# Sparse attention and two expert layers in one kernel: one run of value matmuls per group and head pair, shared turns of the last keys, and later weights moved by DMA before they are turned

## The chip, the core and the metric

One core of one Trainium2 chip runs the whole kernel. The metric is the device time of one execution in microseconds (us). The engines are named as in the profile: PE (matrix products; PEld is its weight load), DVE, ACT, POOL and SP. DVE, ACT and POOL work elementwise, and SP issues every DMA of this kernel, one after the other.

## What is computed

Batch 2, 8 heads, 576 tokens, head size 64, all fp32. Each row of scores keeps its 32 largest.

```python
scores = scale * np.matmul(q, k.transpose(0, 1, 3, 2))
kth = np.partition(scores, -32, axis=-1)[..., -32:-31]
scores = np.where(scores >= kth, scores, -1e9)
attn = softmax(scores)                      # by rows, 1e-9 added to the sum
x = (attn @ v)                              # heads side by side: 1152 x 512
x = sum(p[:, e:e+1] * (relu(x @ w1[e]) @ w2[e]) for e in range(4))    # 512 -> 1024 -> 512
out = ((x @ w_a) * (x @ w_b)) @ w_out       # 512 -> 1536 -> 512
```

## The kernel before

The 1152 tokens are nine tiles of 128: four of each batch (512 tokens), and one, `MIX`, with the last 64 tokens of both. The tiles form four groups of 1, 2, 3 and 3 tiles, called groups 0 to 3 here. The attention is done group by group, in a group by head pair (4 of them), in a head pair by tile: 36 steps, each of one tile and two heads. Steps 0 to 3 are group 0, 4 to 11 group 1, 12 to 23 group 2, 24 to 35 group 3.

A step does this. PE makes the scores of the two heads (`scores`), ACT copies them out of PSUM (L703). DVE finds the 32 largest of each row in four rounds of eight, MAX8 (L723) with MATCH_REPLACE8 between them (L731), which writes the tile `e`. Then POOL (L748), ACT (L754), POOL (L758), ACT (L762), POOL (L767), DVE (L770) and ACT (L773) make the softmax weights in `e`. `weigh` turns each head's weights on PE (L461) in five pieces: four of 128 keys and one of the last 64, whose turned form has 64 partitions. ACT copies the turned weights out of PSUM into a slot of `pts` in two instructions (L828, L832). Last, PE multiplies them with v, ten products of fp32 (each two PE instructions) for a tile; the two heads write the two halves of the 128 partitions, so these matmuls have 64 weight columns, and the trace shows their shape as 128*64. The products of the last 64 keys read `vrem`. After a group's last tile of a head pair, ACT and DVE copy the result to `xs` (L866, L868).

As soon as all head pairs of a group are done, its expert layer can begin (`plain` for group 0, `experts` for the others). An expert weight unit is loaded to `raw`, split into two fp32r parts by ACT (L889) and POOL or DVE (L890) into `mid`, and used by PE; ACT (L959) and DVE (L963, L988) take the results out. The last layer (`gated`) follows when all groups are through.

The order on every engine is worked out before the launch by a planner (`Plan`). Each operation has an engine, an assumed duration, a key (the smallest goes first among those that could run), what it waits for, and the slots of memory that it holds. Attention has keys near its step's number and the expert layers keys above 500 (for PE above 1000), so expert work fills what attention leaves free. The order found is emitted as it stands, one queue per engine, so a waiting instruction holds up everything behind it on that engine; that goes for SP's DMAs too. Copies out of PSUM for the expert layers have key -1000 and go before the search for the largest.

Slots that matter here: `e` has six of one head each, so three steps; `pt` has three of one head each; `raw` and `w` have four weight units each. Nothing of the weights is moved by DMA before the change. Turns of q and k are fp32r, turns of the weights are fp32.

Of the kernel before, what the change touches and what calls it, by code (L numbers as in the profile page):

```python
# [319 lines left out]
TURN_R, TURN_F, TOP, REPLACE = 88, 109, 662, 732  # L320
LATE = 2

FILL = 9
SLACK = 1200

# [3 lines left out]
def body(tc, q, k, v, probs, w1, w2, wa, wb, wo, out):  # L329
# [55 lines left out]
    krem = [big.t[0:REM, b * 1024:(b + 1) * 1024].rearrange("p (h a d) -> p h a d", a=2, d=D) for b in range(B)]  # L385
    big.at = 2048
# [4 lines left out]
    big.at = 2048  # L391
# [5 lines left out]
    low = Region("low", 12300, F32)  # L397
# [4 lines left out]
    es = low.slots("e", 6, S)  # L402
    pts = low.slots("pt", 3, (M4 + 1) * 128)
# [117 lines left out]
    krem_done, vrem_done, qrem_done, kept = {}, {}, [], {}  # L521

    def keys(b, h2, key, eng):
# [11 lines left out]
        if b not in krem_done:  # L535
            rr = krraws.tile(key)
            rrv = lambda: rr.ap[0:REM].rearrange("p (h d) -> p h d", d=D)

            krem_done[b] = {}
            for h0, h1 in ((0, 2), (2, H)) if first_ else ((0, H),):  # L540
                l2 = load(
                    lambda h0=h0, h1=h1: rrv()[:, h0:h1], lambda h0=h0, h1=h1: last_rows(k, b)[:, h0:h1],
                    key - 1.98 if h1 == 2 else key - 1.9, (), [rr], 16384 * (h1 - h0),
                )
                d = split(
                    lambda h0=h0, h1=h1: krem[b][:, h0:h1, 0], lambda h0=h0, h1=h1: krem[b][:, h0:h1, 1],
                    lambda h0=h0, h1=h1: rrv()[:, h0:h1], 64 * (h1 - h0), key + (0.01 if h0 == 0 else 0.05), [l2], [rr], eng,
                )
                krem_done[b].update({i: d for i in range(h0, h1)})
        got = []  # L550
        for j in range(2):
            at = atts.tile(key + 0.02 + 0.01 * j)

            def turn(j=j, at=at):
                p = at.ap.bitcast(F32R)
                for m in range(M4):
                    tr(p[:, 0, m * 128:(m + 1) * 128], sv()[:, j, m].rearrange("p a d -> p (a d)"), identr)
                tr(p[:, 1, 0:REM], krem[b][:, h + j].rearrange("p a d -> p (a d)"), identr[0:REM, 0:REM])

            o = tensor(640, turn, key + 0.02 + 0.01 * j, sp[j] + krem_done[b][h + j] + [ready], [at, st_])  # L560
            if first_ and j == 1:
                got.append(vector(
                    dve(S),
                    lambda j=j, at=at: nc.vector.tensor_copy(kt.ap[:, j * S:(j + 1) * S], at.ap.rearrange("p a n -> p (a n)")[:, 0:S]),
                    -902 + j, [o], [at, kt],
                ))
                continue
            got.append(scalar(
                S,
                lambda j=j, at=at: nc.scalar.activation(  # L570
                    kt.ap[:, j * S:(j + 1) * S], at.ap.rearrange("p a n -> p (a n)")[:, 0:S], AF.Copy
                ),
                -902 + j, [o], [at, kt],
            ))
# [14 lines left out]
    def start_pair(c, h2, n):  # L589
# [74 lines left out]
        for b in batches(tiles):  # L664
            vt = vts.tile(n)
            pair.v[b] = vt
            pair.vd[b] = [load(
                lambda vt=vt: vt.ap.rearrange("p (h m d) -> p h m d", h=2, m=M4), lambda b=b: main_rows(v, b, h), n - 2.5, (), [vt], since=9e3 + 3e3 * n,
            )]
            if b not in vrem_done:  # L670
                vrem_done[b] = load(lambda b=b: vrem[b][0:REM], lambda b=b: last_rows(v, b), n - 2.4, (), (), 131072, since=14e3)
# [36 lines left out]
    def masked(sd, n):  # L708
# [5 lines left out]
        e = [es.tile(n) for _ in range(2)]  # L714
        last, firsts = [], []

        def top(x, src, c0, rounds, width, key, done):

            for r in range(rounds):
# [4 lines left out]
                    [m8, sd[x][0], e[x]],  # L724
# [3 lines left out]
                if r < rounds - 1:  # L728
                    done = vector(
                        132 + 1.04 * width,  # L730
                        lambda at=at, cs=cs: nc.vector.match_replace(  # L731
                            out=src[1](), in_to_replace=m8v()[:, x, cs], in_values=at(), imm_value=LOW
                        ),
                        key + 0.02 * r + 0.01, [done], [m8, sd[x][0], e[x]],
                    )
            return done

        for x in range(2):
            s = sd[x][0]
            key = n + (0.4 if urgent else 0.001) * x  # L740
            last.append(top(x, [lambda s=s: s.ap, lambda x=x: e[x].ap], 0, TOPK // 8, S, key, sd[x][1]))
# [8 lines left out]
        for x in range(2):  # L750
# [3 lines left out]
                S, lambda x=x, s=s: nc.scalar.activation(e[x].ap, s.ap, AF.Relu, bias=endv()[:, x, 1:2], scale=-STEEP),  # L754
                ks, [en], [s, e[x], ends], sbuf=True, ptr=True,
            )
            b = gpsimd(
                pool_(S), lambda x=x, s=s: nc.gpsimd.tensor_tensor(e[x].ap, s.ap, e[x].ap, op=ALU.subtract), ks, [a], [s, e[x]]  # L758
# [4 lines left out]
                    e[x].ap, e[x].ap, AF.Exp, bias=endv()[:, x, 0:1], scale=scale, accum_out=sums.ap[:, x:x + 1]  # L763
                ),
                ks, [b], [e[x], ends, sums], sbuf=True, ptr=True, extra=92,
# [5 lines left out]
        for x in range(2):  # L771
            out_.append((e[x], scalar(
                S, lambda x=x: nc.scalar.activation(e[x].ap, e[x].ap, AF.Copy, scale=sums.ap[:, x:x + 1]),  # L773
                ks, [rc], [e[x], sums], sbuf=True, ptr=True,
            )))
        return out_

    def hurried(sd, n, m8v, m8, ends, endv, sums, firsts, last):

        out_ = []  # L780
        for x in range(2):
            s, e = sd[x][0], es.tile(n)
# [5 lines left out]
                S, lambda x=x, s=s, e=e: nc.scalar.activation(e.ap, s.ap, AF.Exp, bias=endv()[:, x, 0:1], scale=scale),  # L788
# [4 lines left out]
            def mask(x=x, s=s, e=e, sv=sv):  # L793
                nc.vector.scalar_tensor_tensor(  # L794
                    e.ap, s.ap, m8v()[:, x, TOPK - 1:TOPK], e.ap, op0=ALU.is_ge, op1=ALU.mult, accum_out=sv()
# [3 lines left out]
                nc.vector.tensor_scalar(e.ap, e.ap, sv(), None, op0=ALU.mult)  # L799

            out_.append((e, vector(1450, mask, -3000, [ex, last[x]], [s, e, m8, sums], port=True)))
        return out_
# [3 lines left out]
    def weigh(pair, i, ed, n):  # L806

        t, T = pair.tiles[i], pair.T
        if i == 0:
            pair.o, pair.od = os_.tile(), []  # L810
        ov = lambda: pair.o.ap[:, 0:T * 128].rearrange("p (t c) -> p t c", c=128)
        pt, ptd = [], []
        for e, done in ed:

            kt = n + (-0.45 if n == URGENT else 0.5)
            at, p = atts.tile(kt), pts.tile(n)

            def turn(e=e, at=at):
                a = at.ap.rearrange("p b (m c) -> p (b m) c", c=128)
# [4 lines left out]
            o = tensor(4 * TURN_F + 80, turn, kt, [done, ready], [at, e])  # L824

            def ev0(at=at, p=p):
                a = at.ap.rearrange("p b (m c) -> p (b m) c", c=128)
                nc.scalar.activation(p.ap[:, 0:MAIN].rearrange("p (m c) -> p m c", c=128), a[:, 0:M4], AF.Copy)  # L828

            def ev1(at=at, p=p):  # L830
                a = at.ap.rearrange("p b (m c) -> p (b m) c", c=128)
                nc.scalar.activation(p.ap[0:REM, MAIN:MAIN + 128], a[0:REM, M4], AF.Copy)  # L832

            ke = -3000 if n == URGENT else -900
            ptd.append(scalar(512, ev0, ke, [o], [at, p]))
            ptd.append(scalar(128, ev1, ke, [o], [at, p]))
            pt.append(p)
        groups = [(0, 128, t[0])] if t != MIX else [(b * REM, (b + 1) * REM, b) for b in range(B)]
        bs = [b for _, _, b in groups]

        def emit():

            for r0, r1, b in groups:
                for m in range(M4 + 1):
                    for j in range(2):
                        vt = pair.v[b].ap.rearrange("p (h m d) -> p h m d", h=2, m=M4)
                        l = vt[:, j, m] if m < M4 else vrem[b][:, pair.h + j]
                        mm(
                            ov()[j * D:(j + 1) * D, i, r0:r1], l, pt[j].ap[:, m * 128 + r0:m * 128 + r1],
                            start=(m == 0), stop=(m == M4),  # L850
                        )

        pair.od.append(tensor(
            1245, emit, n + 0.6, [zeroed] + ptd + sum((pair.vd[b] for b in bs), []) + [vrem_done[b] for b in bs], [pair.o] + pt + [pair.v[b] for b in bs]
        ))
# [380 lines left out]
```

## Time and profile before

| | |
|---|---|
| time, median of 3 runs | 841.81 us (841.73 to 843.05) |
| span of the profiled execution | 838.8 us |
| what lies around the span, against the median | 3.0 us |
| PE busy | 816.7 us, 97% |
| PEld busy | 730.4 us, 87% |
| DVE busy | 702.5 us, 84% |
| ACT busy | 540.0 us, 64% |
| POOL busy | 265.7 us, 32% |
| DMA queue | 116.17 MB, 43.9% of 16 engines |
| mean granted PE clock | 0.997 |

The span runs from the first to the last instruction of the profiled execution; that execution's own time is its span and what lies around it, taken here as the 3.0 us between span and median. Busy time is a mean over stages with different limits: the attention's steps end about half way through, and what is left is PE work.

### The profile page before, as it was taken

To read this page: it belongs to the slowest core of one execution; us is meant where nothing else is said; L and a number is where in the kernel's file an instruction comes from. 1 tells how busy PE (TensorE), PEld (TensorE's weight loads), DVE (VectorE), ACT (ScalarE), POOL (GpSimd) and SP (SyncE) were. 2 spreads that over 40 slices of the span, in tenths; PEclk is the share of its full clock that TensorE was granted. 3 is DMA by queue.
4 is the path that set the end of the run, shared out by engine and by line. 5 is a ranking of instruction groups with operands and counts; after the bars stand their busy time and mean duration, and the time that the engine had idled before them with its cause. 6 is when DMAs were issued, how large, how long until landed. Compare 5 with 4: busy or idle time off the path is not lost.

```text
span 838.8 us, 14118 instructions
## 1 busy us (share of the span) xinstructions
PE 816.7 (97%) x5177; PEld 730.4 (87%) x5177; DVE 702.5 (84%) x1363; ACT 540.0 (64%) x1037; POOL 265.7 (32%) x250
## 2 busy tenths in 40 slices
PE   7599999999999999999999999999999999999997
PEld 6477877789898999899989998999898989999996
DVE  7999999999999999999969998545235888899723
ACT  6888887989999989887666556343125535344220
POOL 3634443797998966763110000000000000000000
PEclk9999999999999999999999999999999999999999
DMA  5849977754555435233335656433002322323003
GB/s 176 286 120 313 308 240 236 218 175 165 192 172 178 148 138 182 84 95 101 101 126 169 208 158 220 126 125 101 1 1 63 89 78 73 101 78 100 26 1 113
DMA packets 83509, 117.06 MB, mean 140 GB/s; under 512 B 10608, under 2 KB 54640, under 8 KB 83440
## 3 DMA queue, kind: packets, MB, share of 16 engines
q1 hardware_dynamic: 83440, 116.17, 43.9%
q8 instruction: 40, 0.66, 0.3%
q14 instruction: 29, 0.24, 0.1%
HBM read 109.07 MB, written 7.08 MB: 138 GB/s over the span
## 4 chain that ended last, share of the span: by engine, by line
PE 80%; DVE 14%; ACT 4%; issue 1%; POOL 0%; DVEq 0%; POOLq 0%; ACTq 0%
PE ps L458 76%; DVE low L723 7%; DVE low L731 6%; PE ps L461 5%; ACT mid L889 1%; ACT low L773 1%; ACT low L762 1%; ACT low L703 0%; ACT low L828 0%; ACT low L754 0%; ACT big L514 0%; ACT big L655 0%; DVE low L794 0%; POOL low L758 0%; DVE low L1175 0%
## 5 line engine op out<-in xcount | busy, mean ns | idle before, releaser
L723 DVE MAX8 low<-low 128x8 f32<-128x576 f32 x288 | 203.3, 745 | 2.8 <-ACT low L703 2.6
L458 PE MATMUL ps<-xs,mid 128*128 128x384 f32 (+1 forms) x1152 | 204.6, 320 | 0.3 <-DVE mid L963 0.2
L458 PE MATMUL ps<-mid 128*128 128x512 f32 x768 | 196.8, 394 | 0.0
L458 PEld LDWEIGHTS ps<-xs,mid 128*128 128x128 f32 x1152 | 184.9, 188 | 9.1 <-DVE xs L1024 0.5
L458 PEld LDWEIGHTS ps<-mid 128*128 128x128 f32 x768 | 140.0, 188 | 22.6
L731 DVE MATCH_REPLACE8 low<-low 128x576 f32<-128x576 f32 x216 | 159.1, 741 | 0.0
L458 PE MATMUL ps<-xs,big 128*128 128x384 f32 x864 | 152.6, 335 | 0.0
L458 PEld LDWEIGHTS ps<-xs,big 128*128 128x128 f32 x864 | 150.2, 188 | 1.5 <-DVE xs L1024 0.3
L889 ACT ACTIVATE mid<-raw 128x1024 fp32r<-128x1024 f32 x96 | 101.7, 1062 | 44.4 <-PE ps L458 33.9
L890 POOL TENSOR_TENSOR mid<-raw,mid 128x1024 fp32r<-128x1024 f32 x48 | 115.2, 2407 | 13.8 <-ACT mid L889 9.5
L758 POOL TENSOR_TENSOR low<-low 128x576 f32<-128x576 f32 x70 | 99.6, 1438 | 31.9 <-ACT low L754 30.4
L890 DVE TENSOR_TENSOR mid<-raw,mid 128x1024 fp32r<-128x1024 f32 x48 | 59.3, 1236 | 24.6 <-ACT mid L889 24.1
L959 ACT ACTIVATE mid<-ps 128x384 fp32r<-128x384 f32 (+1 forms) x96 | 43.8, 457 | 52.5 <-PE ps L458 51.5
L458 PE MATMUL ps<-big,mid 128*128 128x512 f32 x324 | 76.1, 391 | 0.0
L458 PEld LDWEIGHTS ps<-big,mid 128*128 128x128 f32 x324 | 60.5, 188 | 12.6 <-DVE low L1175 0.6
L963 DVE SCALAR_TENSOR_TENSOR mid<-ps,mid 128x384 fp32r<-128x384 f32 (+1 forms) x96 | 48.3, 505 | 25.0 <-ACT mid L959 24.6
L1154 ACT ACTIVATE low<-ps 128x384 f32<-128x384 f32 x36 | 17.7, 492 | 69.7 <-PE ps L458 69.3
L773 ACT ACTIVATE low<-low 128x576 f32<-128x576 f32 x70 | 51.3, 774 | 12.1 <-DVE low L770 12.0
L762 ACT ACTIVATE low<-low 128x576 f32<-128x576 f32 x70 | 54.4, 778 | 2.2 <-POOL low L758 2.1
L461 PE MATMUL ps<-identr,low 128*128 128x128 f32 (+1 forms) x360 | 50.6, 283 | 4.7 <-ACT low L773 4.0
L754 ACT ACTIVATE low<-low 128x576 f32<-128x576 f32 x70 | 52.3, 776 | 4.3 <-POOL low L748 4.3
L703 ACT ACTIVATE low<-ps 128x576 f32<-128x576 f32 x72 | 46.6, 650 | 11.4 <-POOL low L758 7.5
(90 smaller groups left out, 1024.8 us busy)
## 6 DMA issues: line engine op xcount, KB each, us to landing
raw<-in_moe_w_dram SPq DMA_DIRECT2D x122, 512.0 KB, 3.8
big<-kscr SPq DMA_DIRECT2D x20, 576.0 KB, 5.5
low<-in_v_dram SPq DMA_DIRECT2D x24, 256.0 KB, 3.9
low<-in_moe_w_a_dram SPq DMA_DIRECT2D x12, 512.0 KB, 4.3
low<-in_moe_w_b_dram SPq DMA_DIRECT2D x12, 512.0 KB, 3.8
low<-in_moe_w_out_dram SPq DMA_DIRECT2D x12, 512.0 KB, 3.6
kscr<-big SPq DMA_DIRECT2D x8, 576.0 KB, 4.7
ys<-in_moe_w_dram SPq DMA_DIRECT2D x6, 512.0 KB, 5.2
```

The lines of the kernel that those rows point to most:

```text
L458: nc.tensor.matmul(out, l, r, **kw)
L461: nc.tensor.transpose(out, a, i)
L703: S, lambda: nc.scalar.activation(s.ap.rearrange("p (c n) -> p c n", c=2), at.ap[:, :, 0:HALF], AF.Copy),
L723: 62 + 1.04 * width, lambda at=at, cs=cs: nc.vector.max(m8v()[:, x, cs], at()), key + 0.02 * r, [done],
L731: lambda at=at, cs=cs: nc.vector.match_replace(out=src[1](), in_to_replace=m8v()[:, x, cs], in_values=at(), imm_value=LOW),
L754: S, lambda x=x, s=s: nc.scalar.activation(e[x].ap, s.ap, AF.Relu, bias=endv()[:, x, 1:2], scale=-STEEP),
L758: pool_(S), lambda x=x, s=s: nc.gpsimd.tensor_tensor(e[x].ap, s.ap, e[x].ap, op=ALU.subtract), ks, [a], [s, e[x]]
L762: lambda x=x: nc.scalar.activation(e[x].ap, e[x].ap, AF.Exp, bias=endv()[:, x, 0:1], scale=scale, accum_out=sums.ap[:, x:x + 1]),
L773: S, lambda x=x: nc.scalar.activation(e[x].ap, e[x].ap, AF.Copy, scale=sums.ap[:, x:x + 1]),
L889: hi = scalar(1024, lambda: nc.scalar.activation(u.ap[:, 0:1024], r.ap, AF.Copy), 500 + s, [ld], [u, r], sbuf=True)
L890: sub = lambda eng: eng.tensor_tensor(u.ap[:, 1024:2048], r.ap, u.ap[:, 0:1024], op=ALU.subtract)
L963: lambda h=h, p=p: nc.vector.scalar_tensor_tensor(h.ap[:, n:2 * n], p.ap[:, 0:n], 0.0, h.ap[:, 0:n], op0=ALU.max, op1=ALU.subtract),
```

## The change

- The two heads' weights of a step lie in one tile of 1152 columns. The second head's keys are put in another order, its last 64 first (in `keys` too), so that the last 64 keys of both heads are neighbours and are turned together: nine turns for a step, all of 128 columns, and two copies out of PSUM (128x512 and 128x640) in place of four.
- `vrem` holds v of the last keys in the upper partitions for even heads and in the lower ones for odd heads, and zeros elsewhere; a product of the last keys now runs over 128 partitions. Its load is two DMAs of 64 KB.
- The products with v are no longer emitted tile by tile but for all tiles of a group and head pair together, after the last of them.
- From step 8 on (`MOVED`), the weights of a step are moved by two DMAs of 288 KB, one for each head, from `e` into a slot of the new fp32r buffer `er`, and turned from there as fp32r.
- `e` has three slots of two heads (as much memory as before), `pt` four of two heads, `er` two. `er` lies over `krem` and `kspl`, of which the planner lets it have a slot when the keys are done, and the weights of the last layer come there after it.

```diff
+AV, SWITCH = 1092, 350
+MOVED = 8
...
+    ers = big.slots("er", 2, 2 * S)
+    ers.rank = 0.5
...
-    es = low.slots("e", 6, S)
-    pts = low.slots("pt", 3, (M4 + 1) * 128)
+    es = low.slots("e", 3, 2 * S)
+    pts = low.slots("pt", 4, 2 * S)
...
-            nc.gpsimd.memset(vrem[b][REM:128], 0.0)
-        for p in pts.aps:
-            nc.gpsimd.memset(p[REM:128, MAIN:MAIN + 128], 0.0)
+            for j in range(2):
+                nc.gpsimd.memset(vrem[b][(1 - j) * REM:(2 - j) * REM, j::2], 0.0)
...
-                tr(p[:, 1, 0:REM], krem[b][:, h + j].rearrange("p a d -> p (a d)"), identr[0:REM, 0:REM])
+                r = p[:, 0, MAIN - REM:MAIN] if j else p[:, 1, 0:REM]
+                tr(r, kremv(b)[:, h + j].rearrange("p a d -> p (a d)"), identr[0:REM, 0:REM])
...
+        (e, done), p, ptd = ed, pts.tile(n), []
+        f, idt = e, ident
+        if n >= MOVED:
+            f, idt = ers.tile(n), identr
+            done = [load(
+                lambda j=j: f.ap[:, j * S:(j + 1) * S].bitcast(F32), lambda j=j: e.ap[:, j * S:(j + 1) * S], n + 0.1, [done[j]], [e, f], S * 512,
+            ) for j in range(2)]
...
+                if j:
+                    tr(a[:, MAIN - 128:MAIN], f.ap[:, MAIN:MAIN + 128], idt)
                 for m in range(M4):
-                    tr(a[:, m], e.ap[:, m * 128:(m + 1) * 128], ident)
-                tr(a[0:REM, M4], e.ap[:, MAIN:S], ident)
+                    c0 = j * (S + REM) + m * 128
+                    tr(a[:, j * MAIN + m * 128:j * MAIN + (m + 1) * 128], f.ap[:, c0:c0 + 128], idt)
...
+        pair.turned.append((t, p, ptd))
+        if i < T - 1:
+            return
...
-        pair.od.append(tensor(
-            1245, emit, n + 0.6, [zeroed] + ptd + ...
+        pair.od = [tensor(
+            T * AV + SWITCH, emit, n + 0.6, [zeroed] + sum((d for _, _, d in pair.turned), []) + ...
```

## Rows read from the trace of the kernel before

**Rows 1.** The page's busy tenths in 40 slices of 21 us each.

```profile
PE   7599999999999999999999999999999999999997
...
DVE  7999999999999999999969998545235888899723
```

**Rows 2.** The chain that ended last, in order of time: start, us, what.

```profile
435.15 42.63 PE ps L458 x247
...
479.62 137.13 PE ps L458 x696
```

**Rows 3.** The timeline of PE, end of group 2's attention: start, us, what, count.

```profile
276.69 0.52 PE L458 MATMUL ps<-xs,mid 128*128 128x256 f32 x3
277.13 1.10 PE L458 MATMUL ps<-low 128*64 128x128 f32 x16
...
282.94 0.52 PE L458 MATMUL ps<-xs,mid 128*128 128x256 f32 x3
283.29 2.90 PE L458 MATMUL ps<-mid 128*128 128x512 f32 x12
286.03 1.25 PE L461 MATMUL ps<-identr,low 128*128 128x128 f32 x10
287.04 1.64 PE L458 MATMUL ps<-mid 128*128 128x512 f32 x6
...
289.67 1.09 PE L458 MATMUL ps<-low 128*64 128x128 f32 x16
...
290.92 1.33 PE L458 MATMUL ps<-big,qm 128*128 128x288 f32 x8
292.08 0.63 PE L461 MATMUL ps<-identr,big 128*128 128x128 f32 x6
292.55 0.93 PE L458 MATMUL ps<-mid 128*128 128x512 f32 x3
...
293.78 2.85 PE L458 MATMUL ps<-xs,mid 128*128 128x384 f32 x15
```

**Rows 4.** The timeline of PE, products with v of the last step.

```profile
436.47 0.69 PE L458 MATMUL ps<-low 128*64 128x64 f32 x16
436.99 0.29 PE L458 MATMUL ps<-low,vrem 128*64 128x64 f32 x4
437.11 0.64 PE L458 MATMUL ps<-low 128*64 128x64 f32 x16
437.57 0.29 PE L458 MATMUL ps<-low,vrem 128*64 128x64 f32 x4
437.79 1.65 PE L458 MATMUL ps<-mid 128*128 128x512 f32 x6
```

**Rows 5.** The timelines of DVE, POOL and ACT, weights of step 23.

```profile
270.19 1.41 DVE L723 MAX8 low<-low 128x8 f32<-128x576 f32 x2
...
273.33 0.21 POOL L748 TENSOR_TENSOR low<-low,facs 128x4 f32<-128x4 f32 x1
...
284.72 1.43 ACT L773 ACTIVATE low<-low 128x576 f32<-128x576 f32 x2
```

**Rows 6.** The timeline of all engines, weights of step 11.

```profile
132.14 0.20 POOL L748 TENSOR_TENSOR low<-low,facs 128x4 f32<-128x4 f32 x1 [2.01 <-DVE low L770]
...
141.14 1.44 ACT L773 ACTIVATE low<-low 128x576 f32<-128x576 f32 x2 [0.75 <-DVE low L770]
```

**Rows 7.** DMA issues by line: count, KB each, median us to landing.

```profile
big<-kscr SPq DMA_DIRECT2D x20, 576.0 KB, 5.5
...
low<-in_v_dram SPq DMA_DIRECT2D x24, 256.0 KB, 3.9
...
out_dram<-low SPq DMA_DIRECT2D x8, 256.0 KB, 2.0
```

**Rows 8.** The timelines of PE (turns of step 15) and DVE (step 18).

```profile
198.61 0.71 PE L461 MATMUL ps<-identr,low 128*128 128x128 f32 x5
...
201.37 0.76 DVE L723 MAX8 low<-low 128x8 f32<-128x576 f32 x1 [0.79 <-ACT low L703]
```

More of the change, by code (lines that the diff above doesn't have):

```diff
@@ L384, in body @@
     big = Region("big", 10752, F32R)
-    krem = [big.t[0:REM, b * 1024:(b + 1) * 1024].rearrange("p (h a d) -> p h a d", a=2, d=D) for b in range(B)]
-    big.at = 2048
+    krems = big.slots("krem", B, 1024)
     kspls = big.slots("kspl", 1, 2 * M4 * 2 * D)
@@ L390, in body @@
     qts = big.slots("qt", 2, 3 * 256)
-    big.at = 2048
+    big.at = 0
+    ers = big.slots("er", 2, 2 * S)
+    ers.rank = 0.5
     mid = Region("mid", 4 * 2048 + 5 * 768, F32R)
@@ L396, in body @@
     wraws = raw.slots("wraw", 4, 1024)
-    low = Region("low", 12300, F32)
+    low = Region("low", 12300 + 4 * 1152 - 3 * 640, F32)
     kraws = low.slots("kraw", 2, 2 * M4 * D)
@@ L521, in body @@
     krem_done, vrem_done, qrem_done, kept = {}, {}, [], {}
+    krem = [krems.tile(b) for b in range(B)]
+    kremv = lambda b: krem[b].ap[0:REM].rearrange("p (h a d) -> p h a d", a=2, d=D)
     def keys(b, h2, key, eng):
@@ L556, in turn @@
                 for m in range(M4):
-                    tr(p[:, 0, m * 128:(m + 1) * 128], sv()[:, j, m].rearrange("p a d -> p (a d)"), identr)
-                tr(p[:, 1, 0:REM], krem[b][:, h + j].rearrange("p a d -> p (a d)"), identr[0:REM, 0:REM])
-            o = tensor(640, turn, key + 0.02 + 0.01 * j, sp[j] + krem_done[b][h + j] + [ready], [at, st_])
+                    tr(p[:, j, m * 128:(m + 1) * 128], sv()[:, j, m].rearrange("p a d -> p (a d)"), identr)
+                r = p[:, 0, MAIN - REM:MAIN] if j else p[:, 1, 0:REM]
+                tr(r, kremv(b)[:, h + j].rearrange("p a d -> p (a d)"), identr[0:REM, 0:REM])
+            o = tensor(640, turn, key + 0.02 + 0.01 * j, sp[j] + krem_done[b][h + j] + [ready], [at, st_, krem[b]])
             if first_ and j == 1:
@@ L670, in start_pair @@
             if b not in vrem_done:
-                vrem_done[b] = load(lambda b=b: vrem[b][0:REM], lambda b=b: last_rows(v, b), n - 2.4, (), (), 131072, since=14e3)
+                vrem_done[b] = [
+                    load(lambda b=b, j=j: vrem[b][j * REM:(j + 1) * REM, j::2], lambda b=b, j=j: last_rows(v, b)[:, j::2], n - 2.4, (), (), 65536, since=14e3)
+                    for j in range(2)
+                ]
         return pair
@@ L713, in masked @@
         urgent = n == URGENT
-        e = [es.tile(n) for _ in range(2)]
+        ep = es.tile(n)
+        ev = lambda x: ep.ap[:, x * S:(x + 1) * S]
         last, firsts = [], []
@@ L723, in top @@
                     62 + 1.04 * width, lambda at=at, cs=cs: nc.vector.max(m8v()[:, x, cs], at()), key + 0.02 * r, [done],
-                    [m8, sd[x][0], e[x]],
+                    [m8, sd[x][0], ep],
                 )
@@ L733, in top @@
                         ),
-                        key + 0.02 * r + 0.01, [done], [m8, sd[x][0], e[x]],
+                        key + 0.02 * r + 0.01, [done], [m8, sd[x][0], ep],
                     )
@@ L740, in masked @@
             key = n + (0.4 if urgent else 0.001) * x
-            last.append(top(x, [lambda s=s: s.ap, lambda x=x: e[x].ap], 0, TOPK // 8, S, key, sd[x][1]))
+            last.append(top(x, [lambda s=s: s.ap, lambda x=x: ev(x)], 0, TOPK // 8, S, key, sd[x][1]))
         if urgent:
@@ L753, in masked @@
             a = scalar(
-                S, lambda x=x, s=s: nc.scalar.activation(e[x].ap, s.ap, AF.Relu, bias=endv()[:, x, 1:2], scale=-STEEP),
-                ks, [en], [s, e[x], ends], sbuf=True, ptr=True,
+                S, lambda x=x, s=s: nc.scalar.activation(ev(x), s.ap, AF.Relu, bias=endv()[:, x, 1:2], scale=-STEEP),
+                ks, [en], [s, ep, ends], sbuf=True, ptr=True,
             )
             b = gpsimd(
-                pool_(S), lambda x=x, s=s: nc.gpsimd.tensor_tensor(e[x].ap, s.ap, e[x].ap, op=ALU.subtract), ks, [a], [s, e[x]]
+                pool_(S), lambda x=x, s=s: nc.gpsimd.tensor_tensor(ev(x), s.ap, ev(x), op=ALU.subtract), ks, [a], [s, ep]
             )
@@ L762, in masked @@
                 lambda x=x: nc.scalar.activation(
-                    e[x].ap, e[x].ap, AF.Exp, bias=endv()[:, x, 0:1], scale=scale, accum_out=sums.ap[:, x:x + 1]
+                    ev(x), ev(x), AF.Exp, bias=endv()[:, x, 0:1], scale=scale, accum_out=sums.ap[:, x:x + 1]
                 ),
-                ks, [b], [e[x], ends, sums], sbuf=True, ptr=True, extra=92,
+                ks, [b], [ep, ends, sums], sbuf=True, ptr=True, extra=92,
             ))
@@ L771, in masked @@
         for x in range(2):
[L772 to L776, printed above, removed]
+            out_.append(scalar(
+                S, lambda x=x: nc.scalar.activation(ev(x), ev(x), AF.Copy, scale=sums.ap[:, x:x + 1]),
+                ks, [rc], [ep, sums], sbuf=True, ptr=True,
+            ))
+        return ep, out_
     def hurried(sd, n, m8v, m8, ends, endv, sums, firsts, last):
-        out_ = []
+        out_, e = [], es.tile(n)
+        ev = lambda x: e.ap[:, x * S:(x + 1) * S]
         for x in range(2):
-            s, e = sd[x][0], es.tile(n)
+            s = sd[x][0]
             en = gpsimd(
@@ L791, in hurried, with mask @@
             sv = lambda x=x: sums.ap[:, x:x + 1]
-            def mask(x=x, s=s, e=e, sv=sv):
+            def mask(x=x, s=s, sv=sv):
                 nc.vector.scalar_tensor_tensor(
-                    e.ap, s.ap, m8v()[:, x, TOPK - 1:TOPK], e.ap, op0=ALU.is_ge, op1=ALU.mult, accum_out=sv()
+                    ev(x), s.ap, m8v()[:, x, TOPK - 1:TOPK], ev(x), op0=ALU.is_ge, op1=ALU.mult, accum_out=sv()
                 )
@@ L798, in mask @@
                 nc.vector.reciprocal(sv(), sv())
-                nc.vector.tensor_scalar(e.ap, e.ap, sv(), None, op0=ALU.mult)
-            out_.append((e, vector(1450, mask, -3000, [ex, last[x]], [s, e, m8, sums], port=True)))
-        return out_
+                nc.vector.tensor_scalar(ev(x), ev(x), sv(), None, op0=ALU.mult)
+            out_.append(vector(1450, mask, -3000, [ex, last[x]], [s, e, m8, sums], port=True))
+        return e, out_
     xdone = {}
@@ L809, in weigh @@
         if i == 0:
-            pair.o, pair.od = os_.tile(), []
+            pair.o, pair.turned = os_.tile(), []
         ov = lambda: pair.o.ap[:, 0:T * 128].rearrange("p (t c) -> p t c", c=128)
[L812 to L819, printed above, removed]
-                for m in range(M4):
-                    tr(a[:, m], e.ap[:, m * 128:(m + 1) * 128], ident)
-                tr(a[0:REM, M4], e.ap[:, MAIN:S], ident)
[L824 to L837, printed above, removed]
@@ L838, in weigh @@
-        groups = [(0, 128, t[0])] if t != MIX else [(b * REM, (b + 1) * REM, b) for b in range(B)]
-        bs = [b for _, _, b in groups]
-        def emit():
[L843 to L851, printed above, removed]
@@ L853, in weigh @@
-        pair.od.append(tensor(
-            1245, emit, n + 0.6, [zeroed] + ptd + sum((pair.vd[b] for b in bs), []) + [vrem_done[b] for b in bs], [pair.o] + pt + [pair.v[b] for b in bs]
-        ))
+        (e, done), p, ptd = ed, pts.tile(n), []
[5 more added lines that the diff above has]
+            ) for j in range(2)]
@@ new lines, in weigh, with turn @@
+        kt = n + (-0.45 if n == URGENT else 0.5)
+        ke = -3000 if n == URGENT else -900
+        for j in range(2):
+            at = atts.tile(kt)
+            def turn(j=j, at=at):
+                a = (at.ap if f is e else at.ap.bitcast(F32R)).rearrange("p b n -> p (b n)")
+                if j:
+                    tr(a[:, MAIN - 128:MAIN], f.ap[:, MAIN:MAIN + 128], idt)
+                for m in range(M4):
+                    c0 = j * (S + REM) + m * 128
+                    tr(a[:, j * MAIN + m * 128:j * MAIN + (m + 1) * 128], f.ap[:, c0:c0 + 128], idt)
+            hold = (M4 + j) * TURN_F if f is e else 46 + (M4 + j - 2) * 85 + 64
+            o = tensor(hold, turn, kt, [done[j], done[0], ready], [at, f])
+            w = MAIN + j * 128
+            ptd.append(scalar(
+                w, lambda j=j, w=w, at=at: nc.scalar.activation(
+                    p.ap[:, j * MAIN:j * MAIN + w], at.ap.rearrange("p b n -> p (b n)")[:, j * (MAIN - 128):j * (MAIN - 128) + w], AF.Copy
+                ), ke, [o], [at, p],
+            ))
@@ new lines, in weigh @@
+        pair.turned.append((t, p, ptd))
+        if i < T - 1:
+            return
+        def emit():
+            for i, (t, p, _) in enumerate(pair.turned):
+                for r0, r1, b in [(0, 128, t[0])] if t != MIX else [(b * REM, (b + 1) * REM, b) for b in range(B)]:
+                    vt = pair.v[b].ap.rearrange("p (h m d) -> p h m d", h=2, m=M4)
+                    for m in range(M4 + 1):
+                        for j in range(2):
+                            l = vt[:, j, m] if m < M4 else vrem[b][:, pair.h + j]
+                            c0 = j * (S + REM) + m * 128 if m < M4 else MAIN
+                            mm(ov()[j * D:(j + 1) * D, i, r0:r1], l, p.ap[:, c0 + r0:c0 + r1], start=(m == 0), stop=(m == M4))
@@ L856, in weigh @@
+        bs = batches(pair.tiles)
+        pair.od = [tensor(
+            T * AV + SWITCH, emit, n + 0.6, [zeroed] + sum((d for _, _, d in pair.turned), []) + sum((pair.vd[b] + vrem_done[b] for b in bs), []),
+            [pair.o] + [p for _, p, _ in pair.turned] + [pair.v[b] for b in bs],
+        )]
         if i == T - 1:
@@ L1220 @@
     import concourse.bass_utils as bu
-    nc = bacc.Bacc("TRN2", target_bir_lowering=False, num_devices=1)
+    nc = bacc.Bacc("TRN2", target_bir_lowering=False, num_devices=1, dynamic_dma_scratch_size=1024)
     arrays, args = {}, []
```

10 lines of the change are left out of this document (5 added, 5 removed).

## The prediction

> **What bounds the kernel now.** I read the page's slices first, then the chain that ended last, then PE's timeline where one group of tiles ends. The slices show two engines full at once: from the third slice (42 us) PE shows a nine throughout, and DVE does so up to the 21st (440 us), where the attention ends [rows 1]. So there are two candidates, and which one counts changes on the way. The chain says which at the end: from 435 us on it is PE alone, with nothing between its pieces but PE itself [rows 2]. PE time saved there would be time saved. Before 440 us the reader has to look at what PE lives on while attention is waited for, the expert matmuls of the group before.
>
> PE's timeline at the end of group 2 shows that [rows 3]. The last products with v of group 2 begin at 289.67. At 292.55 come three 128x512 matmuls of group 1's experts, the last of them, and at 293.78 the first 128x384 matmuls of group 2's experts. PE's supply of old work ends within a microsecond of the moment at which the new work becomes possible. Up to here PE time is matched by attention time, and attention time is DVE time: DVE is full since the first slices [rows 1], and the change takes nothing off it. After this point PE has a stock: group 3's attention ends at about 438 [rows 4], while group 2's experts last until 478, where their result is turned [rows 2]. That is 40 us of work in hand. So I split the gain at 294 us: what PE saves after it counts in full, what it saves before it counts only if attention of group 2 comes sooner.
>
> **The change, part by part.**
>
> *Turns.* The ten fp32 turns of a step take 1.01 us, from 286.03 to 287.04 [rows 3]. Six fp32r turns of q take 0.47 (292.08 to 292.55), so 0.078 each and nine 0.70. A moved step saves 0.31, and 28 steps 8.7 us; 12 of them (24 to 35) lie after 294 us and make 3.7. In steps 0 to 7 one turn of ten goes, 0.10 for each, 0.8 us. They lie in the part that DVE sets, and I count nothing for them.
>
> *Products with v.* Their number and shape stay, and so does their time inside a run. What goes is the change of shape around each run. Three 128x256 matmuls ahead of one take 0.44 to the next start (276.69 to 277.13), the same three ahead of a full-width matmul 0.35 [rows 3]: 0.09 on entering. The last step, which has two such sequences in a row, shows the rest: its first 16 instructions take 0.52 and the second 16 take 0.46, the last four inside the run 0.12 and those at its end 0.22 [rows 4]. That makes 0.06 and 0.10, in all 0.25 for a run. There were 36 runs and there will be 16, so 20 x 0.25 = 5.0 us, of which 4 head pairs x 2 x 0.25 = 2.0 lie after 294 us.
>
> Here a rule speaks on the turns too. By the shape of the weights, the turns of the last 64 keys are also half-width, so two of the ten in a run could each cost a change of shape. Rows show no such cost: ten in 1.01 leaves 0.10 for each [rows 3]. The Trainium skill (TensorEngine Tiling, Key Properties) says that changing the tiling mode drains the engine; by it the removal of 24 half-width turns after 294 us would give another 24 x 0.25 = 6.0 us and a sum of 832.1. The row disagrees with that for turns, and I go by the row.
>
> *Copies out of PSUM.* Two ACT instructions in place of four. ACT ends nothing in the chain's last half [rows 2]; it hides behind PE and DVE, and I count nothing. It is some help to the part before 294 us, and stands in what I give back there.
>
> *The moves.* 56 DMAs of 288 KB. Before the change no weights are moved, so the time is bounded by the nearest rows: 2.0 us for a write of 256 KB, 5.5 for a read of 576 KB; a load of 256 KB in SBUF rows like these takes 3.9 [rows 7], and I take that. Reading cannot start until the weights are done, so a move adds 2.0 to 5.5 us between L773 and the turn of each step from 8 on. The Trainium skill (DMA: Bandwidth & Descriptors, Anatomy of one DMA) gives some 2.0 us fixed and bytes at 436 GB/s for DMAs of the GpSimd path, so an estimate of 2.7 for this size; with it the sum would be 836.9. On SP the moves stand in one queue with the weight loads; a move that waits for L773 holds up the loads behind it. The planner puts both where it expects them to be free, and four raw and four split units lie ahead of PE, so a wait of a few microseconds is hidden. Without that cover it would cost PE its whole length.
>
> *The way through the end of a group.* It gets longer by the move, 3.9, and by the products of the first two tiles, which now stand between the last turn and the result. A tile takes 1.25 (289.67 to 290.92) [rows 3], less the 0.16 of first and last, 1.09; so 2.2. In all 6.1 us (4.2 to 7.7). Part of it is given back. PE has 8.8 us less to do before 294 (14.5 in all less 5.7), so the old expert work runs out earlier, and with it the ACT and POOL work that its weights need; then the way is clearer. How much clearer shows in two steps. In step 23 DVE ends at 271.6 and L748 begins at 273.33, 1.7 later; from there to L773 at 284.72 are 11.4 us [rows 5]. In step 11, ahead of which no weights were being split, that same stretch took 9.0 (132.14 to 141.14) [rows 6]. So 1.7 + 2.4 = 4.1 can come back (bounds 0 and 6.1). I take 4.1, and group 2's experts begin 2.0 us later than now. At the end of group 3 the same 6.1 us fall into the 40 us of stock and cost nothing; if the stock were gone they would cost 6.1.
>
> *Slots.* `e` holds three steps as before, but a pair is free when its second move has landed. I count nothing where that is sooner than three steps; where it isn't, a rival below has it. `zeros`, the loads of `vrem` and the new place of the last keys in `keys` move a few instructions of the first 60 us that nothing waits for; 0 either way, at most the tenths of a microsecond that they take.
>
> **The sum.** The profiled execution took its span of 838.8 and 3.0 around it, 841.8, which is the median shown. 841.8 - 3.7 - 2.0 + 2.0 = 838.1; I say 838.
>
> **Rivals.**
>
> *All that PE saves is saved.* For it: PE shows nines all the way from 42 us [rows 1], and a new order may put attention ahead of expert work, since the planner weighs many orders. Against: old work ends just as new work begins [rows 3], with DVE full. Without the parts that lie before group 1's experts start (0.8, four moved steps 1.2, four head pairs of two tiles 1.0), 11.5 of 14.5 us count: 830.3.
>
> *The longer way is not given back.* The copies, splits and scores stand in the way as before. 841.8 - 5.7 + 6.1 = 842.2, no change.
>
> *Slower: DVE waits for a free pair of `e`.* Step 15's last turns start at 198.61 and end by 199.1; three steps later DVE starts at 201.37 and writes that slot 0.8 us after, a margin of 3.1 us [rows 8]. A move of 3.9 eats it and 0.8 more. From the point at which a pair is held longer than three steps of DVE, each further microsecond is lost to DVE, and before 294 us nothing makes up for it. For the six crowded steps 14 to 19 that is 5 us, and a clogged way gives nothing back: 841.8 - 5.7 + 6.1 + 5 = 847. Against: a pair need no longer wait for PE's turn, and other steps have more room.
>
> *Half-width turns drained after all:* 832, against the row.
>
> **How the numbers follow.** 838 (own range 834 to 841) 0.42; all of PE's saving, 830, 0.22; not given back, 842, 0.15; slower, 844 to 848, 0.18; drained turns, 832, 0.03. A measurement of this kernel can tell about 0.2% from no change, 1.7 us: faster is below 840.1, slower above 843.5. Faster takes 0.37 of the first case, and the second and last: 0.62. Same takes the rest of the first, most of the third and the edge of the slower one: 0.19, which leaves 0.19. The range reaches from 829, which holds most of the second case, to 846, which leaves the far end of the slower one.
>
> **What would show it.** Nine turns in 0.70 us from step 8 on; 16 runs with v, three tiles in 3.4 to 3.5 us; moves landing in 2 to 5.5 us; PE idle for some microseconds ahead of group 2's first 128x384 matmuls, and these at 294 to 298; from there to the end about 5.7 us less than now. I would be wrong if those matmuls begin well before 292 (then DVE did not set the point), if DVE shows idle time for a slot before 294, or if PE waits for weights behind a move.

## The result: 0.96% slower, and the profile after

The changed kernel takes 848.54 us (median of 4 runs, 848.00 to 852.34), the kernel before, beside it on the same chip, 841.77. The ratio is 1.0096 (95% interval 1.0083 to 1.0109). The forecast was 838.0, range 829 to 846: wrong in sign, and outside the range.

The profiled execution is the 852.34 one, 3.8 above the median, with a span of 850.4; so the traces differ by 11.6 us where the medians differ by 6.8. PE's busy time fell, 816.7 to 809.0. Its idle time, span less busy time, rose from 22.1 to 41.4. That is -7.7 + 19.3 = 11.6: the saving on PE is there, and new idle time is 2.5 times as large. Most of it lies between 60 and 300 us. Windows of the kernel before (us; PE, PEld, DVE, ACT and POOL busy; PE clock, DMA share, GB/s):

```profile
0.00:60.00 60.00, 44.06 (x291) 36.90 (x291) 54.76 (x125) 46.06 (x101) 24.80 (x44) 0.97 0.61 189
60.00:300.00 240.00, 238.44 (x1804) 202.97 (x1806) 238.21 (x512) 217.01 (x439) 172.96 (x147) 1.00 0.68 217
300.00:470.00 170.00, 170.00 (x1185) 153.49 (x1182) 159.84 (x305) 130.93 (x251) 67.92 (x61) 1.00 0.38 121
```

The same windows of the kernel after:

```profile
0.00:60.00 60.00, 41.01 (x281) 33.94 (x282) 54.79 (x122) 44.43 (x91) 24.49 (x42) 0.80 0.60 185
60.00:300.00 240.00, 224.63 (x1673) 189.48 (x1672) 226.31 (x488) 203.53 (x373) 165.37 (x138) 0.99 0.76 242
300.00:470.00 170.00, 167.54 (x1231) 151.36 (x1230) 154.37 (x297) 129.44 (x235) 77.80 (x70) 0.98 0.52 168
```

From 60 to 300 us PE's idle time went from 1.6 to 15.4 us and DVE's from 1.8 to 13.7. Every engine did less there. No engine became the bound; all of them wait more. In the first 60 us PE idles 3.0 us more, and the mean granted clock there is 0.80 in place of 0.97. The page's slices, to set beside [rows 1], show the nines broken for both engines:

```profile
PE   6589989899999989999999999999999999999997
DVE  7999998988999999999995999845334898899723
```

The waits of the kernel after from 60 to 460 us say for what (us in total, times, longest). Here are lines of PE's, ACT's and DVE's:

```profile
PE ps L464 <- DMA big<-low: 5.4, 9, 1.4
PE ps L461 <- ACT low L1083: 4.8, 6, 1.3
ACT low L848 <- PE ps L464: 14.7, 17, 2.4
ACT low L711 <- POOL low L767: 11.5, 8, 4.1
DVE low L732 <- ACT low L711: 7.3, 6, 2.9
```

In the kernel before, DVE's wait for the score copy came to 1.1 us and ACT's for the turned weights to 1.0. One step shows how a late move gets to DVE: the weights of step 12, and the scores of step 15. Timelines of ACT, SP, PE and DVE, kernel after:

```profile
161.39 0.79 ACT L782 ACTIVATE low<-low 128x576 f32<-128x576 f32 x1
...
162.21 0.92 SPq L443 DMA_DIRECT2D big<-low  x1
...
169.37 0.54 PE L464 MATMUL ps<-identr,big 128*128 128x128 f32 x4 [1.42 <-DMA big<-low]
...
171.44 0.61 PE L464 MATMUL ps<-identr,big 128*128 128x128 f32 x5
171.90 0.77 PE L461 MATMUL ps<-big 128*128 128x288 f32 x4
...
172.09 0.71 ACT L848 ACTIVATE low<-ps 128x640 f32<-128x640 f32 x1 [0.60 <-PE ps L464]
172.76 0.65 ACT L711 ACTIVATE low<-ps 128x576 f32<-128x576 f32 x1
...
173.44 0.76 DVE L732 MAX8 low<-low 128x8 f32<-128x576 f32 x1 [2.90 <-ACT low L711]
```

The second head's move is issued at 162.21, when its weights are done (L782), and lands 9.2 us later. PE's five turns start at 171.44, and the score product of step 15 (171.90) stands behind them. Its copy (L711) starts at 172.76, and DVE, with nothing to search, has waited 2.90 us.

That step 15 has to wait for step 12 stands in the kernel. The turns of step n have the key n + 0.5 and the scores of step n+3 the key n + 0.6 (their step's number less `AHEAD`, 2.4), and both take one of the same two places in PSUM (`att`), which are given out in the order of the keys. So the weights of each step lie on a loop: weights, turns, scores of the third step after it, DVE. From the end of the weights of step 12 to the first score copy of step 15 are 172.76 - 162.18 = 10.6 us here. In the kernel before (timeline of ACT) they are 156.78 - 152.53 = 4.3:

```profile
151.07 1.46 ACT L773 ACTIVATE low<-low 128x576 f32<-128x576 f32 x2
...
156.78 0.67 ACT L703 ACTIVATE low<-ps 128x576 f32<-128x576 f32 x1
```

Over steps 8 to 23 the median of this way is 3.8 us before and 7.4 after, longer by about one landing. Before, the first score copy of a step starts 5.4 us (median) ahead of the moment at which DVE is done with the step in front; after, 2.2.

The chain that ended last goes through that move, and through three others of 4 to 8 us before it (start, us, what):

```profile
112.40 4.17 DMA big<-low
...
125.08 7.53 DMA big<-low
...
147.41 5.77 DMA big<-low
...
162.21 9.19 DMA big<-low
171.44 0.61 PE ps L464 x5
```

The way through step 23, to set beside [rows 3, 5]. Timelines of DVE, POOL, ACT, SP and PE, kernel after:

```profile
284.43 1.41 DVE L732 MAX8 low<-low 128x8 f32<-128x576 f32 x2
...
287.57 0.19 POOL L757 TENSOR_TENSOR low<-low,facs 128x4 f32<-128x4 f32 x1
...
296.08 0.70 PE L461 MATMUL ps<-xs,mid 128*128 128x384 f32 x3
...
298.50 1.44 ACT L782 ACTIVATE low<-low 128x576 f32<-128x576 f32 x2
...
299.30 1.14 SPq L443 DMA_DIRECT2D big<-low  x2
...
302.85 0.63 PE L464 MATMUL ps<-identr,big 128*128 128x128 f32 x4 [0.31 <-DMA big<-low]
304.21 0.87 PE L464 MATMUL ps<-identr,big 128*128 128x128 f32 x5 [0.73 <-DMA big<-low]
...
308.02 1.97 PE L461 MATMUL ps<-low 128*64 128x128 f32 x16
...
312.32 1.33 PE L461 MATMUL ps<-big,qm 128*128 128x288 f32 x8
```

DVE ends the step at 285.84, 14.2 later than before. The way from there to the last product's end takes 312.32 - 285.84 = 26.5 us, against 290.92 - 271.6 = 19.3: 7.2 longer. The prediction had 6.1 for the longer way, less 4.1 that was to come back. From the start of the weights' last part (L782) on, the way is 13.8 us in place of 6.2, so 7.6 longer; 0.9 of that is the products of three tiles, which take 4.3 us at a mean granted clock of 0.79, after PE had idled 2.4 us from 300 us on, against 3.4 in e2. From L757 to L782 it is 10.9 in place of 11.4: 0.5 comes back, not 4.1. And the prediction had nothing for the 14.2.

These 14.2 us are 11.4 of DVE's idle time and 2.8 of its work. From 60 us to the end of step 23 DVE idles 13.2 us in place of 1.7, 6.8 of them for scores (L711) and 4.3 for results of group 0's experts that PE is late with (L1097, L1099). It is busy for 212.7 us in place of 209.9, as it does more expert work by then.

### The profile page after: what moved, and what is told of

It reads as the page before. It is cut to its first block, busy times and chain, and to the rows that moved or that the text cites. A ratio compares the mean times of both kernels' runs of the same rounds, so it can differ in the third digit from the quotient of the medians.

```text
span 850.4 us, 14131 instructions
## 1 busy us (share of the span) xinstructions
PE 809.0 (95%) x5141; PEld 722.3 (85%) x5141; DVE 704.8 (83%) x1363; ACT 534.8 (63%) x965; POOL 267.7 (31%) x249
## 4 chain that ended last, share of the span: by engine, by line
PE 78%; ACT 10%; DMA 6%; DVE 2%; POOL 2%; issue 1%; SPq 1%; POOLq 0%; ACTq 0%
PE ps L461 74%; DMA big<-low 5%; PE ps L464 4%; ACT low L782 2%; DMA raw<-in_moe_w_dram 1%; ACT mid L905 1%; ACT low L771 1%; ACT low L763 1%; ACT low L711 1%; POOL mid L906 1%; DVE low L732 1%; ACT big L660 1%; DVE low L740 1%; SPq L443 1%; ACT big L516 1%
## 5 line engine op out<-in xcount | busy, mean ns | idle before, releaser
L464 PEld LDWEIGHTS ps<-identr,big 128*128 128x128 f32 (+1 forms) x476 | 51.2, 143 | 31.0 <-issue 7.8
L464 PE MATMUL ps<-identr,big 128*128 128x128 f32 (+1 forms) x476 | 61.2, 258 | 13.4 <-DMA big<-low 5.4
L763 ACT ACTIVATE low<-low 128x576 f32<-128x576 f32 x70 | 52.2, 779 | 12.6 <-POOL low L757 12.6
L711 ACT ACTIVATE low<-ps 128x576 f32<-128x576 f32 x72 | 47.0, 655 | 19.4 <-POOL low L767 11.5
L848 ACT ACTIVATE low<-ps 128x512 f32<-128x512 f32 x72 | 46.5, 653 | 17.7 <-PE ps L464 17.6
```

Source lines behind the costliest of these rows:

```text
L464: nc.tensor.transpose(out, a, i)
L711: S, lambda: nc.scalar.activation(s.ap.rearrange("p (c n) -> p c n", c=2), at.ap[:, :, 0:HALF], AF.Copy),
L763: S, lambda x=x, s=s: nc.scalar.activation(ev(x), s.ap, AF.Relu, bias=endv()[:, x, 1:2], scale=-STEEP),
L848: w, lambda j=j, w=w, at=at: nc.scalar.activation(p.ap[:, j * MAIN:j * MAIN + w], at.ap.rearrange("p b n -> p (b n)")[:, j * (MAIN - 128): ...
```

## The experiments

Medians, with the ratio to the kernel before run beside each. What follows is from one profiled execution of each kernel: its time, idle times (240 us less the busy time of the window from 60 to 300 us), DVE's end of step 23, and the way from the end of a step's weights to the first score copy of the third step after it (median over steps 8 to 23).

| kernel | us | ratio (95%) | profiled | PE idle | DVE idle | step 23 | way to scores |
|---|---|---|---|---|---|---|---|
| before | 841.8 | | 841.8 | 1.6 | 1.8 | 271.6 | 3.8 |
| after: moves from step 8 | 848.5 | 1.0096 (1.0083 to 1.0109) | 852.3 | 15.4 | 13.7 | 285.8 | 7.4 |
| e2: no moves | 840.7 | 0.9997 (0.9987 to 1.0006) | 841.5 | 8.0 | 3.3 | 269.4 | 3.7 |
| e7: no moves, products by tile | 842.5 | 1.0014 (1.0004 to 1.0023) | 843.9 | 4.7 | 4.7 | 272.6 | 3.9 |
| e4: moves from 24 | **837.6** | 0.9954 (0.9939 to 0.9969) | 837.9 | 7.0 | 2.2 | 269.0 | 3.7 |
| e8: moves from 24, products by tile | 841.5 | 1.0004 (0.9994 to 1.0014) | 841.3 | 4.3 | 1.9 | 271.7 | 3.6 |
| e12: moves from 16 | 841.9 | 1.0011 (1.0001 to 1.0020) | 841.9 | 8.1 | 7.4 | 279.8 | 5.5 |
| e9: moves in 8 to 23 alone | 849.5 | 1.0096 (1.0076 to 1.0117) | 849.3 | 14.6 | 12.1 | 285.0 | 7.6 |
| e3: moves from 8, products by tile | 846.4 | 1.0045 (1.0028 to 1.0062) | 854.1 | 12.1 | 17.8 | 291.8 | 7.7 |
| e5: four pairs in `e` | 847.8 | 1.0071 (1.0056 to 1.0086) | 847.6 | 15.4 | 9.7 | 281.2 | 7.7 |
| e1: order of after, no moves | 846.1 | 1.0050 (1.0031 to 1.0070) | 843.2 | 13.0 | 6.7 | 278.5 | 7.1 |
| e6: fp32r from ACT, no moves | 843.1 | 1.0018 (1.0009 to 1.0028) | 843.1 | 9.7 | 9.3 | 282.7 | 3.5 |
| e11: planner adds 2.5 us to a landing | 853.6 | 1.0152 (1.0130 to 1.0175) | 856.5 | 12.9 | 17.3 | 294.0 | 9.8 |
| e10: moves issued by ACT | 865.5 | 1.0287 (1.0270 to 1.0304) | 866.1 | 19.1 | 20.3 | 292.4 | 7.7 |

Every kernel with a way of 7 us or more is slower than every one with less than 6. The other columns don't follow the time one for one: e2 idles 6.4 us more on PE than the kernel before and is no slower, and e6 ends step 23 13.3 us later than e2 and is 2.4 slower.

**e1, the order of after without its moves.** The order stays as it was worked out for moves; ACT writes the fp32r slot. One head of step 27 is overwritten by step 28, and the weights are rounded by ACT.

```diff
-  nc.scalar.activation(ev(x), ev(x), AF.Copy, ...)
+  nc.scalar.activation(fts[n].ap[:, x * S:(x + 1) * S] if n >= MOVED else ev(x), ev(x), AF.Copy, ...)
...
+            for o in done:
+                o.emit = lambda: None
```

> The changed kernel with its order of every engine kept as it is, but without the 56 moves: L782 writes the weights of steps 8 to 35 straight into the fp32r slot (rounded on the way; one head of step 27 is overwritten by step 28, so the output differs there). What goes is the landing, its place in SP's queue and its traffic, nothing else. Theory A (PE waits at the head of its queue for moves, scores behind them come late, DVE stands idle): 836 to 842, PE waits for moves gone, DVE's idle time between 100 and 300 us halved or better. Theory B (the longer way through the run of products at the end of a head pair): 845 to 849. Theory C (the new order and the slots of two heads are worse by themselves): 846 to 849.

By the medians only 2.4 of after's 6.8 us come back, by the ratios 3.9. The runs spread, 843.16 to 847.17, and the profiled one is the fastest. PE still idles 13.0 us in the window. This is what theories B and C gave; A fails. An order that leaves room for 28 moves is slow even where nothing has to land: the way to the scores stays 7.1 us.

**e2, no moves; e3, products by tile, with moves.**

```diff
-MOVED = 8
+MOVED = 99
```

> The changed kernel with no step moved (all turns fp32, nine to a step), its order worked out anew. Theory A: 838 to 841, that is 841.8 less 2.0 for the eight runs of products gone after 294 us, less 1.2 for twelve turns gone there, and nothing lost before. Theory B: 845 to 849, as the run of products stays. Theory C: 845 to 849.

```diff
-        if i < T - 1:
-            return
...
-        pair.od = [tensor(T * AV + SWITCH, emit, ...
+        pair.od = pair.od + [tensor(AV + 150, emit, ...
```

> The changed kernel with the products with v emitted tile by tile again, moves kept. Theory A: 847 to 852, the moves' waits stay and 5 us of PE time come back of which some 2 count. Theory B: 840 to 843. Theory C: 846 to 850.

Without moves the loss is gone, as theory A alone had it. With moves and products by tile most of it stays, against theory B. So the moves, or an order made for them, are needed for it, and the run of products is not its cause.

**e4, moves in the last twelve steps; e5, a fourth pair for `e` (the region `low` is made larger for it).**

```diff
-MOVED = 8
+MOVED = 24
```

> The changed kernel with moves in steps 24 to 35 alone, where PE has group 2's experts in hand. Theory A: 835 to 839, as a late turn costs nothing there and 12 steps save 0.3 each, 3.7 us, on top of the kernel without moves. Theory B: 845 to 849. Theory C: 843 to 849.

```diff
-    low = Region("low", 12300 + 4 * 1152 - 3 * 640, F32)
+    low = Region("low", 12300 + 5 * 1152 - 3 * 640, F32)
...
-    es = low.slots("e", 3, 2 * S)
+    es = low.slots("e", 4, 2 * S)
```

> The changed kernel, moves from step 8, with four slots of two heads for e in place of three (the region low is made larger). Theory D1 (the move keeps a pair of e longer than three steps allow, and the order is spread for want of a slot): 838 to 842, and DVE ends step 23 at 269 to 274 us as it does without early moves. Theory D2 (the move lengthens the way of a step, and the order worked out with it has ACT and POOL instructions stand in front of others they should not; slots are not short): 845 to 849, step 23 ends at 281 or later.

e4 beats both kernels: 3.1 below e2, where the prediction had 3.7 for those twelve steps' turns. With e5 the loss stays, and DVE's wait for scores is as long as in after:

```profile
DVE low L732 <- ACT low L711: 7.7, 6, 2.3
```

That refutes slots of `e` as the main cause: a fourth pair takes 0.8 us off.

**e6, fp32r weights written by ACT.** No moves, and the order worked out for it; the weights are rounded by ACT.

```diff
+        f = ers.tile(n) if n >= MOVED else ep
...
-  nc.scalar.activation(ev(x), ev(x), AF.Copy, ...)
+  nc.scalar.activation(f.ap[:, x * S:(x + 1) * S], ev(x), AF.Copy, ...)
```

> The changed kernel with weights of steps 8 to 35 written by L782 straight into the fp32r slot, no moves, and the order worked out anew for that (weights are rounded to fp32r on the way). The way of a step is as short as before, and the turns are the cheap ones. Theories A, D1 and D2, all of which blame the move: 833 to 838, step 23 ends by 272 us. If the fp32r slot er or the cheap turns spoil the order by themselves: 843 or more.

A miss for every theory that blames the move: all 28 cheap turns and no move, and still 843.1, which just meets the last alternative. DVE ends step 23 at 282.7. The way to the scores is short here, 3.5. What is late are the weights of single steps, up to 26.8 us after DVE's end of the step (23.4 at most before). Why this order has them late, and is 2.4 above e2, these runs don't settle.

**e7 and e8, products by tile with e2's and e4's moves** (e3's edit, with `MOVED` 99 and 24).

> No moves, and the products with v tile by tile: of the change only the shared turns and the pairs of heads stay. Against 840.7 for the same with the run of products: if the runs are worth their 2 us behind 294 us, 842 to 844; if the longer way at the end of a head pair costs as much as the runs save, 839 to 842.

> Moves in steps 24 to 35 alone, and the products with v tile by tile. Against 837.55 for the same with the run of products: 839 to 841 if the eight runs saved behind 294 us count in full (2.0 us) and more of them before; 836 to 838 if they don't.

One run of products for a group and head pair is worth 842.5 - 840.7 = 1.8 us without moves and 841.5 - 837.6 = 4.0 with the late ones. The prediction had 2.0. With moves from step 8 it is the other way round: there products by tile are 2.1 faster (e3). e8 ends 0.5 above the range expected for it.

**e9, moves in steps 8 to 23 alone; e10, moves issued by ACT.**

```diff
-        if n >= MOVED:
+        if MOVED <= n < 24:
```

> The changed kernel with moves in steps 8 to 23 alone, steps 24 to 35 turned from e as fp32. If the harm of the moves lies ahead of group 2's experts (16 early steps) and their good behind it: 848 to 853, worse than all of the change, with DVE ending step 23 at 280 us or later. If the harm is spread evenly over all moved steps: 843 to 846.

```diff
-            done = [load(
-                lambda j=j: f.ap[...].bitcast(F32), lambda j=j: e.ap[...], n + 0.1, [done[j]], [e, f], S * 512,
+            done = [plan.add(
+                "ACT", 470, lambda j=j: nc.scalar.dma_start(out=f.ap[...].bitcast(F32), in_=e.ap[...]), n + 0.1, [done[j]], [e, f], lag=3000,
```

> The changed kernel with its moves issued by ACT, on ACT's own DMA ring, in place of SP's, where they stand behind expert weights of 512 KB. ACT pays some 0.47 us for each. Theory A2 (early moves land late, 7 to 9 us, because they stand behind weight loads, and PE, ACT and DVE pass the lateness on): landings of 2 to 4 us even between 100 and 170 us, 840 to 845. If the time the move takes at its shortest is enough, or the order does it: 846 to 851.

e9 has all of the loss: it lies with the early moves. Its steps show where. Against e2, DVE ends step 11 only 0.2 us later, step 19 13.9 and step 23 15.6. In steps 8 to 11 the weights are done some 10 us after DVE's end of the step (median 9.7), and the longer way is absorbed; in steps 12 to 19, beside the expert work of group 1, they take 16.5, and it is not.

e10 was a miss: taken out of SP's queue, the moves land no sooner. Its DMA issue by line, then after's (KB each, median us to landing):

```profile
big<-low ACTq DMA_DIRECT2D x56, 288.0 KB, 4.8
```

```profile
big<-low SPq DMA_DIRECT2D x56, 288.0 KB, 3.7
```

PE's wait for them grew from 5.4 to 19.1 us:

```profile
PE ps L464 <- DMA big<-low: 19.1, 21, 2.2
```

The issues stand in ACT's queue too, and the planner set aside 56 x 0.47 = 26 us of ACT for them, so e10 doesn't separate the landing from ACT's load.

**e11, a planner that adds 2.5 us to each move's landing.**

```diff
-    def add(..., lag=100, nbytes=0, port=False):
+    def add(..., lag=0, nbytes=0, port=False):
...
-                    end = dma_free + LAND
+                    end = dma_free + LAND + op.lag
...
+            for o in done:
+                o.lag = 2500
```

> The changed kernel with the planner told that a move lands 2.5 us later than it assumes, so that turns are put later in PE's queue. Theory A2: PE's waits for moves go from 5.4 us to under 2 and the time to 842 to 846. If lateness of the landing is not what slows attention: 846 to 851.

Waits at the head of PE's queue for a move go, as expected: 1.0 us is left of 5.4. The time rises by 5.1, above both ranges expected. A line of its DVE's waits:

```profile
DVE low L732 <- ACT low L711: 11.8, 11, 3.6
```

What PE no longer waits for a move, DVE waits for scores. So the loss is not what PE loses at the head of its queue. It comes with the length of the way, whether the order leaves room for it or not: told 2.5 us more, the order makes the way to the scores 2.4 longer, 9.8.

**e12, moves from step 16.**

```diff
-MOVED = 8
+MOVED = 16
```

> Moves from step 16 on: eight moved steps (16 to 23) lie in the part of the attention in which nothing is in stock, twelve (24 to 35) in the part with some 40 us of stock. Theory A, each moved step without stock makes its group's end later: moves in none, 24 to 35, and 8 to 35 gave 840.7, 837.5 and 848.5 us, so sixteen early steps cost 11.0, and eight cost about half: 841 to 845, with DVE's end of step 23 (269.0 with moves from 24, 285.8 with moves from 8) at 273 to 281. Theory B, the harm comes from the first moved steps alone (8 to 15, where the place of the keys has just been given up): 837 to 839, and step 23 as early as with moves from 24 on, 268 to 271. Theory C, it is group 2's steps alone that count: as with moves from 8 on, 847 to 850, step 23 at 284 to 288.

841.9 and 279.8 are what the first theory gave. None, 8 and 16 early moved steps on top of the late ones take 837.6, 841.9 and 848.5: 0.54 us for each of steps 16 to 23, 0.83 for each of 8 to 15. The way to the scores lies between, too: 5.5.

## Why the prediction was wrong

**The step that failed** is the way through the end of a group: "group 2's experts begin 2.0 us later than now", the only cost that the sum had for the moves. It counted the longer way once, where group 2 ends, took 4.1 of its 6.1 us as given back, and said of the 16 moved steps up to there that a wait of a few microseconds is hidden. It took DVE's pace for given: DVE was full, so step 23 would end at 271.6 whatever happened behind it. But DVE was full only because scores reached it in time, and what happens behind a step's search decides when the scores of the third step after it are made. The move takes up the spare time of that loop, 5.4 us at the median. Step 23 ends 14.2 us later, and of the longer way through the group's end 0.5 comes back in place of 4.1. The size shows between e2 and e9, which differ by the early moves and their turns alone: 849.5 - 840.7 = 8.8 in place of 2.0.

The mark that was to show the 2.0 was met and means nothing: the first 128x384 matmuls of group 2's experts begin at 296.08, 2.3 later than before. They take the first three head pairs only; what needs the last one has to wait for the products that end at 312.32.

**Terms that held.** The turns after 294 us: 3.7 foreseen, 3.1 measured (e2 to e4). Products in one run: 2.0 foreseen, 1.8 and 4.0 measured where no early step is moved. PE time saved before 294 us gains nothing that shows: e6 has cheap turns in steps 8 to 23, and no gain, though its order is late for a reason that is open. The 40 us of stock cover the late moves: in e4 DVE ends the attention 8.6 us later than in e2, and the kernel is 3.1 faster. The two parts that lie late and the new layout, together, are e4: 837.6, the time forecast for all of it.

**The landing** was bounded by 2.0 and 5.5 us. The median is 3.7, as taken (3.9), but six of the 56 take longer than 5.5. And the way depends on the late ones: of the four in the chain shown three take 4.2 to 7.5, and one 9.2. The estimate of 2.7 by the Trainium skill (DMA: Bandwidth & Descriptors, Anatomy of one DMA), which is for DMAs of the GpSimd path, lies between the quickest move, 2.3, and the median.

**The rivals.** "DVE waits for a free pair of `e`" gave 847, near the measured time, by luck: a fourth pair gives 847.8 (e5). It looked for the right thing, a spare time of a few microseconds over three steps, at the wrong place: DVE does idle, but for scores and for results of PE, not for a slot. "All that PE saves is saved" falls with the result itself. "Not given back" was right in what it says of the way, and its 842.2 fell short because it, too, left step 23 where it was. Half-width turns draining would have given some 6 us wherever they go; e7, which has the new layout and turns and little else, gains nothing (1.0014). That speaks for the row, and against the use that the prediction made of the Trainium skill's rule (TensorEngine Tiling, Key Properties) for these turns.

**What stays open.** With the order fixed, taking the landings out gives back 2.4 to 3.9 us (e1); the rest of the early loss is in the order itself, which keeps the scores behind turns that it expects late. That the loop closes through the keys and the two places of `att` is read from the kernel and the traces: no run has a third place, or puts the scores ahead of the turns. Each kernel has an order of its own, and no kernel was run with several; e6, 2.4 above e2 without a longer way, hints at how much of a single difference may be the draw.

## What to carry to other kernels

Where several engines are full in one stage and nothing is in stock, a latency added to a loop that feeds back through in-order queues is not hidden by "a few units lie ahead". Look for the loop in the order and in the places that its parts share, and set the latency against the spare time of each turn of it, not once against its end. Put a saving that costs latency where there is stock: here twelve late steps gained 3.1 us and sixteen early ones lost 11.0. An engine that is busy all the time isn't proven to set the pace: look at how narrowly its input arrives, and what that input has to wait for.

## What the runs showed of the hardware

A move of 288 KB within SBUF landed 2.3 to 9.2 us after its issue, median 3.7. Issued by ACT, off the queue of the weight loads, it landed no sooner: the median is 4.8. Between 158 and 172 us, where the two slowest of them lie, the DMA engines are 80% busy and a weight load of 512 KB takes 7.7 us, against 4.0 over the whole run. That the load on the DMA engines makes them late is not shown: the landings were compared and not tested by themselves.
